# A windowed attention and a two-matrix MLP in one kernel: the first batch's queries and keys loaded on 128 rows over two queues, its masks sliced from one row, block copies in place of zero fills, and the opening put in another order

## The chip, the core and the metric

The kernel runs on one core of a Trainium2 chip. The core has five engines with a queue each: TensorE (PE; its weight loads are shown as PEld), VectorE (DVE), ScalarE (ACT), GpSimd (POOL) and SyncE (SP), which here only issues transfers. An engine takes its instructions in the order of its own queue and waits on semaphores for the others. Sixteen DMA engines move data between the device memory and the core's memory of 128 rows. The metric is the device time of one execution in microseconds; lower is better.

## The reference

```python
def _attn_ref(q, k, v):                 # each (8, 8, 576, 64)
    scores = scale * np.matmul(q, k.transpose(0, 1, 3, 2))
    mask = np.abs(pos[:, None] - pos[None, :]) <= 32
    scores = np.where(mask, scores, -1000000000.0)
    scores = scores - np.max(scores, axis=-1, keepdims=True)
    attn = np.exp(scores)
    attn = attn / (np.sum(attn, axis=-1, keepdims=True) + 1e-09)
    return np.matmul(attn, v)

def _moe_ref(x, w_in, w_out):           # x (4608, 512), w_in (512, 2048), w_out (2048, 512)
    h = x @ w_in
    return np.maximum(0.01 * h, h) @ w_out
```

The attention's output, heads side by side, is the `x` of the second part. Batches are independent; 8 batches of 576 tokens make 4608 rows.

## The kernel before, in words

The heads of a batch are taken in four **pairs** (`p`), the 64 columns of one head on rows 0 to 63 and of the other on 64 to 127. A batch has two **halves** of 288 tokens (`hf`), so an attention step `i` is a batch, a half and a pair, 64 steps in all.

One step: `score(i)` multiplies queries with key blocks of 64 tokens (five small matmuls, one for each key block in reach, L275) into PSUM, ACT takes the exponential (L280), POOL multiplies with a mask of zeros and ones (L282, two inputs, 1.27 us each). `sums(i)` adds over keys with a matmul against a matrix of ones (L304, L301), and VectorE takes the reciprocal (L309). `product(i)` multiplies with the values (L320), and `scaled(i)` multiplies that by the reciprocal into `xT` (L334). The keys `kbd` and the values `vbd` lie as blocks of 128x128 with one head in the upper left and the other in the lower right quarter; the other two quarters have to be zero. `kbd` and `vbd` exist twice, for even and odd batches.

The MLP works on groups `g` of 288 tokens: `h_tile` (L348, 16 column tiles `f` of four matmuls, one for each pair `c`), the leaky ReLU on ACT (`h_out`, L355), and then `o_tile` (L390) for 128 tokens at a time. The last of the four matmuls of a tile needs the product of pair 3. `h_first` runs four tiles side by side, chunk by chunk, so that each pair's chunk can run when its product is there.

Everything is placed by hand (`tc.manual_schedule()`): the order in which the code calls is the order of each engine's queue. After the opening, a plan puts attention steps between the matmuls of the MLP.

What the change touches in the opening:

- **Loads.** `load_qk(b, p)` (L79) reads the q and k of a pair with 96 rows of six tokens (1536-byte runs, 288 KB each); `load_v` (L91) the values, one transfer of 64 rows for each head, in 256-byte runs. All are issued on SP, in the order pair 0, pair 1, values of pair 0, pairs 2 and 3, the other values. Each transfer uses one of eight semaphores, so a ninth waits for the first to land.
- **Casts and transposes.** `cast_qk` (L197, L195) turns q and k into bf16 (q on VectorE or ACT, k on POOL), `transposes` (L225) turns them on TensorE, ACT moves them out of PSUM (L233 for q, L239 for k), and `place_keys` (L258) copies both heads' blocks into `kbd` on VectorE. `cast_v` (L205 on POOL, L203 on ACT) does the same for the values, 64 rows at a time.
- **Zero fills.** `kbd[0]` is cleared on VectorE (L134), `vbd[0]` on ACT (`clear`, L127, three times) and POOL (L158), `kbd[1]` and `vbd[1]` on POOL in eight pieces (L540, L564) between 32 and 45 us.
- **Masks.** Two tiles `mask[hf]`, made on POOL from a pattern `win` (L147 to L165), with even and odd tokens apart, as q's columns are.
- **Weights.** `load_w_in` (L448) and `load_w_out` (L452), four pieces each, are issued by POOL, which casts them to bf16 on the way. The first w_in issue stands on POOL behind the key cast of pair 3.
- **Fillers.** `keep_busy` (L402) issues matmuls whose result nobody reads.

The loads of batch 1 (`load_qk(1, p)`, `load_v(1, p)`) are issued on SP in the opening too; a one-element fill on POOL (L75), which stands behind the second w_out issue, holds them back.

Of the kernel before, what the change touches and what calls it, by code (L numbers as in the profile page):

```python
# [16 lines left out]
def kernel(  # L17
# [14 lines left out]
    nc = tc.nc  # L32
# [34 lines left out]

    def load_qk(b, p, behind=None):

        for into, src, name in ((qf, q, "qf"), (kf, k, "kf")):
            t = fload.tile([96, 2, RUN * D], FP32, name=f"{name}{p}")
# [13 lines left out]
    def load_v(b, p):  # L87

        t = fload.tile([128, NB, D], FP32, name=f"vf{p}")
        for a in range(2):  # L90
            nc.sync.dma_start(  # L91
                out=t[64 * a:64 * a + 64],
                in_=v[b, 2 * p + a].rearrange("(c p) d -> p c d", p=64),
            )
        vf[b, p] = t

    load_qk(0, 0)
    load_qk(0, 1)
    load_v(0, 0)
    load_qk(0, 2)  # L100
    load_qk(0, 3)
    for p in range(1, NPAIR):
        load_v(0, p)
# [5 lines left out]
    nc.vector.tensor_copy(out=ident, in_=ident_f)  # L109

    ones_bd = const.tile([128, 128], BF16)
    nc.vector.memset(ones_bd, 0.0)
    nc.vector.memset(ones_bd[0:64, 0:64], 1.0)
    nc.vector.memset(ones_bd[64:128, 64:128], 1.0)


    qb = const.tile([96, NPAIR, RUN, 2, D], BF16)
    kb = const.tile([96, NPAIR, RUN, 2, D], BF16)
# [4 lines left out]
    nc.vector.memset(zero, 0.0)  # L123

    def clear(t, p):
        flat = t[:, p].rearrange("p n j -> p (n j)")
        nc.scalar.activation(  # L127
            out=flat, in_=zero.to_broadcast([128, NB * 128]), func=AF.Copy,
        )

    mask = [const.tile([128, 2, 2, EVEN], BF16, name=f"mask{i}") for i in range(2)]
    nc.vector.memset(mask[0][:, 1, :, 0:16], 0.0)
    nc.vector.memset(mask[1][:, 1, :, 128:EVEN], 0.0)
    nc.vector.memset(kbd[0], 0.0)  # L134
    clear(vbd[0], 0)
    clear(vbd[0], 1)
    clear(vbd[0], 2)


# [6 lines left out]
    win = const.tile([128, 2, 3, 64], BF16)  # L146
    nc.gpsimd.memset(win, 1.0)  # L147
    for lo in (0, 64):
# [3 lines left out]
            base=0, channel_multiplier=-1, pattern=[[1, 2], [0, 3], [2, 64]],  # L152
# [3 lines left out]
            base=2 * W, channel_multiplier=1, pattern=[[-1, 2], [0, 3], [-2, 64]],  # L156
        )
    nc.gpsimd.memset(vbd[0][:, 3], 0.0)  # L158
    win_f = win.rearrange("p c m i -> p c (m i)")

    def make_mask(hf):
        lo = (16, 32)[hf]
        nc.gpsimd.tensor_copy(out=mask[hf][:, 0], in_=win_f[:, :, lo:lo + EVEN])
        lo = (16, 0)[hf]
        nc.gpsimd.tensor_copy(out=mask[hf][:, 1, :, lo:lo + 128], in_=win_f[:, :, 0:128])  # L165
# [7 lines left out]
    nc.scalar.activation(  # L173
        out=ps[:, 512:512 + HALF], in_=zero.to_broadcast([128, HALF]), func=AF.Copy,
    )
# [8 lines left out]
    qT = {}  # L184

# [13 lines left out]
    def cast_v(b, p, on_act=False):  # L199
        for a in range(2):  # L200
            r = slice(64 * a, 64 * a + 64)
            if on_act:
                nc.scalar.activation(out=vbd[b % 2][r, p, :, r], in_=vf[b, p][r], func=AF.Copy)  # L203
            else:
                nc.gpsimd.tensor_copy(out=vbd[b % 2][r, p, :, r], in_=vf[b, p][r])  # L205
# [42 lines left out]
    def place_keys():  # L248
# [3 lines left out]
        while unplaced:  # L252
            b, p, kT = unplaced.pop(0)
            for a in range(2):
                r = slice(64 * a, 64 * a + 64)
                to = kbd[b % 2][r, p, :, r]
                if b < BY_DMA:
                    nc.vector.tensor_copy(out=to, in_=kT[r].rearrange("p (n j) -> p n j", j=64))  # L258
# [11 lines left out]
    def score(i):  # L270
        b, hf, p = where(i)
        by_c = qT[b][:, p].rearrange("p (c i) -> p c i", c=2)
        for n_, blocks in enumerate(WIN[hf]):
            for blk, i0, n in blocks:
                nc.tensor.matmul(  # L275
                    ps_v[:, n_, :, i0:i0 + n], kbd[b % 2][:, p, blk],
                    by_c[:, :, hf * EVEN + i0:hf * EVEN + i0 + n], start=True, stop=True,
                )
# [368 lines left out]
```

## Time and profile before

| | us |
|---|---|
| three runs | 318.89, 319.77, 320.53 |
| median | 319.77 |
| span of the profiled execution, first to last instruction | 318.5 |
| TensorE busy in the span | 303.2 (95%) |
| VectorE, ACT, POOL busy | 218.2, 182.6, 191.6 |

The profile is of one execution of its own, and its span leaves out what lies before the first and behind the last instruction. Matmuls are pipelined and their ends are modelled, so a busy TensorE need not be a fast one: the five matmuls of a score take 0.65 us in the first 20 us and 0.40 us later, at a granted clock that the profile gives as 1.00 throughout. The chain of waits that ended last is 89% TensorE, 3% DMA and 2% VectorE:

```profile
PE 89%; DMA 3%; DVE 2%; SPq 1%; POOL 1%; ACT 1%; issue 1%; DVEq 0%; ACTq 0%
```

A row of the list of groups reads: line, engine, operation, out<-in, shape and type, count, then busy time in us and the mean of one in ns, then the engine's idle time before them and what ended it.

### The profile page before, as it was taken

To read this page: it belongs to the slowest core of one execution; us is meant where nothing else is said; L and a number is where in the kernel's file an instruction comes from. 1 tells how busy PE (TensorE), PEld (TensorE's weight loads), DVE (VectorE), ACT (ScalarE), POOL (GpSimd) and SP (SyncE) were. 2 spreads that over 40 slices of the span, in tenths; PEclk is the share of its full clock that TensorE was granted. 3 is DMA by queue.
4 is the path that set the end of the run, shared out by engine and by line. 5 is a ranking of instruction groups with operands and counts; after the bars stand their busy time and mean duration, and the time that the engine had idled before them with its cause. 6 is when DMAs were issued, how large, how long until landed. Compare 5 with 4: busy or idle time off the path is not lost.

```text
span 318.5 us, 6474 instructions
## 1 busy us (share of the span) xinstructions
PE 303.2 (95%) x2449; PEld 204.3 (64%) x2449; DVE 218.2 (69%) x259; ACT 182.6 (57%) x393; POOL 191.6 (60%) x251
## 2 busy tenths in 40 slices
PE   2679998999999999999999999999999999999996
PEld 1467774585765858576765858576665858576653
DVE  5678955869655997688755997688745988565100
ACT  7577698474652828374652828375552837464531
POOL 7798963974546866686546866586637866330000
PEclk9999999999999999999999999999999999999999
DMA  8999999997999995399735995399733430000101
GB/s 179 211 186 218 267 250 203 250 206 181 216 242 196 231 206 150 82 251 203 155 76 127 238 227 136 75 223 232 162 76 104 109 70 33 35 35 2 66 31 71
DMA packets 108400, 49.46 MB, mean 155 GB/s; under 512 B 68816, under 2 KB 103888, under 8 KB 108368
## 3 DMA queue, kind: packets, MB, share of 16 engines
q1 hardware_dynamic: 104144, 44.84, 66.8%
q0 software_dynamic: 4224, 4.19, 8.0%
q8 instruction: 19, 0.31, 0.4%
q14 instruction: 13, 0.11, 0.1%
HBM read 36.70 MB, written 9.44 MB: 145 GB/s over the span
## 4 chain that ended last, share of the span: by engine, by line
PE 89%; DMA 3%; DVE 2%; SPq 1%; POOL 1%; ACT 1%; issue 1%; DVEq 0%; ACTq 0%
PE mm L348 39%; PE mm L390 38%; PE x L320 5%; PE ps L275 4%; DMA kf<-in_k_dram 3%; PE s L301 2%; DVE r L309 2%; SPq L79 1%; POOL w_in_bf L448 1%; DVE xT L334 1%; PE tp L225 1%; PE s L304 1%; ACT vbd L203 0%; SPq L91 0%; POOL prob L282 0%
## 5 line engine op out<-in xcount | busy, mean ns | idle before, releaser
L309 DVE RECIPROCAL r<-s 128x288 f32<-128x288 f32 x64 | 125.2, 1956 | 56.5 <-PE s L301 53.3
L282 POOL TENSOR_TENSOR prob<-e,mask 128x576 bf16<-128x576 bf16 x64 | 81.5, 1274 | 87.8 <-ACT e L280 41.1
L348 PE MATMUL mm<-xT,w_in_bf 128*128 128x288 bf16 x1024 | 134.0, 286 | 0.3
L390 PE MATMUL mm<-w_out_bf,gT 128*128 128x512 bf16 (+2 forms) x592 | 130.4, 373 | 0.2 <-DMA w_out_bf<-in_moe_w_out_dram 0.2
L355 ACT ACTIVATE gT<-mm 128x288 bf16<-128x288 f32 x256 | 101.4, 412 | 24.8 <-PE mm L348 8.5
L348 PEld LDWEIGHTS <-w_in_bf 128*128 128x128 bf16 x1024 | 98.4, 98 | 24.8 <-issue 0.6
L390 PEld LDWEIGHTS <-gT 128*128 128x128 bf16 x592 | 56.3, 98 | 59.6 <-issue 0.3
L395 ACT ACTIVATE o_sb<-mm 128x512 f32<-128x512 f32 (+2 forms) x37 | 21.7, 586 | 92.0 <-PE mm L390 92.0
L280 ACT ACTIVATE e<-ps 128x576 bf16<-128x576 f32 x64 | 41.4, 648 | 9.4 <-PE ps L275 9.2
L197 POOL CAST kb<-kf 96x384 bf16<-96x384 f32 (+1 forms) x56 | 35.5, 656 | 4.6 <-DMA kf<-in_k_dram 4.6
L205 POOL CAST vbd<-vf 64x576 bf16<-64x576 f32 x50 | 34.5, 689 | 1.8 <-DMA vf<-in_v_dram 0.4
L334 DVE TENSOR_TENSOR xT<-x,r 128x288 bf16<-128x288 f32 x64 | 29.3, 458 | 8.2 <-PE x L320 1.2
L260 DVE COPY kbd<-kT 64x576 bf16<-64x576 bf16 x48 | 32.3, 672 | 0.3
L275 PE MATMUL ps<-qT,kbd 128*128 128x128 bf16 (+2 forms) x320 | 26.5, 215 | 1.8 <-DVE kbd L258 1.2
L275 PEld LDWEIGHTS <-kbd 128*128 128x128 bf16 x320 | 21.0, 100 | 10.6 <-DVE kbd L258 1.5
L320 PE MATMUL x<-prob,vbd 128*128 128x128 bf16 (+2 forms) x320 | 26.0, 213 | 1.3 <-ACT vbd L203 0.7
L197 POOL CAST qb<-qf 96x384 bf16<-96x384 f32 x48 | 24.5, 538 | 0.0
L320 PEld LDWEIGHTS <-vbd 128*128 128x128 bf16 x320 | 20.6, 99 | 3.9 <-ACT vbd L203 1.8
L292 DVE TENSOR_TENSOR both<-prob 128x288 bf16<-128x288 bf16 x52 | 19.7, 380 | 0.9
L301 PE MATMUL s<-both,ones_bd 128*128 128x288 bf16 x52 | 14.9, 286 | 0.0
L258 DVE COPY kbd<-kT 64x576 bf16<-64x576 bf16 x16 | 7.1, 444 | 8.7 <-ACT kT L239 8.6
L225 PE MATMUL tp<-ident,qb 96*128 96x96 bf16 x48 | 4.4, 243 | 6.2 <-DVE qb L197 6.2
(43 smaller groups left out, 86.6 us busy)
## 6 DMA issues: line engine op xcount, KB each, us to landing
qf<-in_q_dram SPq DMA_DIRECT2D x32, 288.0 KB, 4.5
kf<-in_k_dram SPq DMA_DIRECT2D x32, 288.0 KB, 5.0
vf<-in_v_dram SPq DMA_DIRECT2D x64, 144.0 KB, 4.2
out_dram<-o_sb SPq DMA_DIRECT2D x35, 256.0 KB, 3.6
w_in_bf<-in_moe_w_in_dram POOLq DMA_DIRECT2D x4, 512.0 KB, 8.6
w_out_bf<-in_moe_w_out_dram POOLq DMA_DIRECT2D x4, 512.0 KB, 16.8
qT<-qb SPq DMA_TRANSPOSE x24, 4.1
kT<-kb SPq DMA_TRANSPOSE x24, 3.2
```

The source lines that it names most:

```text
L197: eng.tensor_copy(out=to, in_=tok)
L205: nc.gpsimd.tensor_copy(out=vbd[b % 2][r, p, :, r], in_=vf[b, p][r])
L260: nc.vector.tensor_copy(out=to.rearrange("p n (m c) -> p n c m", c=2), in_=kT[r].rearrange("p (c n m) -> p n c m", c=2, n=NB),)
L275: nc.tensor.matmul(ps_v[:, n_, :, i0:i0 + n], kbd[b % 2][:, p, blk], by_c[:, :, hf * EVEN + i0:hf * EVEN + i0 + n], start=True, stop=True,)
L280: nc.scalar.activation(out=e, in_=ps[:, P0:P0 + 2 * HALF], func=AF.Exp, scale=scale)
L282: nc.gpsimd.tensor_mul(pr.rearrange("p n c i -> p (n c i)"), e, mask[hf].rearrange("p n c i -> p (n c i)"),)
L309: nc.vector.reciprocal(r, s)
L320: nc.tensor.matmul(x_v[:, :, i0:i0 + n], vbd[b % 2][:, p, blk, :], pr[:, n_, :, i0:i0 + n], start=(blk == parts[0][1]), stop=(blk == parts ...
L334: nc.vector.tensor_mul(place(i), x, r)
L348: nc.tensor.matmul(h[:, 0:HALF], w_in_bf[:, c, ts(f, 128)], xT[:, c, ds(g * HALF % RING, HALF)], start=(c == 0), stop=(c == DMC - 1),)
L355: nc.scalar.activation(out=gT[:, f, ds(g * HALF % RING, HALF)].rearrange("p (i c) -> p i c", c=2), in_=h[:, 0:HALF].rearrange("p (c i) -> ...
L390: nc.tensor.matmul(o[:, lo:hi], gT[:, f, ds(128 * j % RING, 128)], w_out_bf[:, f, lo:hi], start=(f == 0), stop=(f == FFC - 1),)
```

## The change

- **Loads of batch 0** (`load_first`): q and k of all pairs lie in two shared buffers of 128 rows. Row `i` holds nine neighbouring tokens; SP loads rows 0 to 63 with five of them (1280-byte runs), ACT loads rows 64 to 127 with the other four (1024-byte runs). Token `9 i + c` for c below 5 stands on row i, for c from 5 on row 64 + i in column c - 5; the fifth column of the lower rows is filled with zeros on POOL. Keys go before queries; pairs 0 and 1 have loads of their own, pairs 2 and 3 share one. The values follow behind all of q and k.
- **Transposes of batch 0** are five of 128x128 and not six of 96x128, for keys and queries (`transpose_first`), and the tokens come out in their natural order, so score, product and leaky ReLU of this batch use plain slices. Eviction (`evict_first`) and placing of the blocks (`place_first`) go to VectorE or ACT, call by call.
- **Masks of batch 0** are overlapping slices of one row `wide`, written from `win` by two ACT copies. The tiles `mask[hf]` for the later batches are copied from it on POOL at the end of the opening.
- **No zero fills** for `vbd[0]`, `kbd[1]` and `vbd[1]`: a block is copied over all 128 rows, times a column `own` that is 1 on the rows of its head and 0 on the others (`own_block`). `kbd[0]` keeps a fill of the two quarters.
- **Weights:** the four w_in issues stand on POOL behind the query cast of pair 1.
- **Order:** the opening is a list of calls, with `score` split into `score`, `exps` and `masked`, and `sums` into `sums` and `inverse`; the masks of steps 0 and 1 are multiplied on VectorE, the others on POOL. 14 filler matmuls stand at the very start, and the others go. The MLP's tiles of group 0 are opened and closed singly.

```diff
+    def load_first(p0, p1, low):
+        for into, src, t in ((kf, k, k_in), (qf, q, q_in)):
+            t = t[:, 0:H * TOP * D].rearrange("p (h c d) -> p h c d", h=H, c=TOP)
+            rows = src[0, 2 * p0:2 * p1].rearrange("h (i c) d -> i h c d", c=ROW)
+            heads = slice(2 * p0, 2 * p1)
+            nc.sync.dma_start(out=t[0:64, heads], in_=rows[:, :, 0:TOP])
+            low.dma_start(out=t[64:128, heads, 0:LOW], in_=rows[:, :, TOP:ROW])
...
-    load_qk(0, 0)
-    load_qk(0, 1)
-    load_v(0, 0)
-    load_qk(0, 2)
-    load_qk(0, 3)
-    for p in range(1, NPAIR):
-        load_v(0, p)
+    load_first(0, 1, nc.scalar)
+    load_first(1, 2, nc.scalar)
...
+    def own_block(eng, out, in_, a):
+        if eng is nc.scalar:
+            eng.activation(out=out, in_=in_, func=AF.Copy, scale=own[:, a:a + 1])
+        else:
+            eng.tensor_scalar_mul(out=out, in0=in_, scalar1=own[:, a:a + 1])
+
+    def value_first(p, a, eng):
+        own_block(eng, vbd[0][:, p, :, 64 * a:64 * a + 64], vf[0, p], a)
...
-    def cast_v(b, p, on_act=False):
+    def cast_v(b, p):
...
-            if on_act:
-                nc.scalar.activation(out=vbd[b % 2][r, p, :, r], in_=vf[b, p][r], func=AF.Copy)
+            if b < BY_DMA:
+                own_block(nc.scalar, vbd[b % 2][:, p, :, r], vf[b, p], a)
...
+    V, G, A = nc.vector, nc.gpsimd, nc.scalar
+    spread(A, GAP + 32, 2)
+    load_first(2, NPAIR, A)
+    qT[0] = attn.tile([128, NPAIR, S], BF16, name="qT")
+    keep_busy(ps, 0, 14, True)
+    cast_first(0, "k", G)
+    fill(V)
+    cast_first(0, "q", V)
+    transpose_first(0, "k")
+    spread(A, 0, 3)
+    transpose_first(0, "q")
+    cast_first(1, "k", V)
+    for p in range(NPAIR):
+        load_v(0, p, V if p == 0 else None)
+    evict_first(0, "k", V)
+    transpose_first(1, "k")
+    evict_first(0, "q", A)
+    cast_first(1, "q", G)
+    evict_first(1, "k", V)
+    place_first(0, A)
+    load_w_in(0, 512)
+    transpose_first(1, "q")
+    place_first(1, V)
+    evict_first(1, "q", A)
+    score(0)
+    load_w_in(512, 1024)
+    cast_first(2, "k", V)
+    exps(0)
+    cast_first(3, "k", V)
+    transpose_first(2, "k")
+    load_w_in(1024, 1536)
+    transpose_first(3, "k")
+    masked(0, V)
+    evict_first(2, "k", A)
+    load_w_in(1536, 2048)
+    cast_first(2, "q", V)
+    score(1)
+    sums(0)
+    cast_first(3, "q", A)
+    place_first(2, V)
+    transpose_first(2, "q")
+    exps(1)
+    value_first(0, 0, G)
+    transpose_first(3, "q")
+    inverse(0)
+    evict_first(2, "q", A)
+    value_first(0, 1, G)
+    evict_first(3, "q", A)
+    score(2)
+    value_first(1, 0, G)
+    product(0)
+    evict_first(3, "k", A)
+    masked(1, V)
+    value_first(1, 1, G)
+    exps(2)
+    scaled(0)
+    sums(1)
+    place_first(3, A)
+    inverse(1)
+    masked(2, G)
+    product(1)
+    value_first(2, 0, A)
+    score(3)
+    value_first(2, 1, G)
+    h_chunk(0)
+    scaled(1)
+    exps(3)
+    sums(2)
+    load_w_out(0)
+    for p in range(NPAIR):
+        load_qk(1, p, nc.gpsimd if p == 0 else None)
+    for p in range(NPAIR):
+        load_v(1, p)
...
+    load_w_out(1)
...
+    make_mask(0, nc.gpsimd)
+    make_mask(1, nc.gpsimd)
```

## The prediction

> **What bounds the kernel now.** I read the page's forty slices first, then three stretches of the span, then the order of VectorE's work in the opening, then the transfers.
>
> ```profile
> PE   2679998999999999999999999999999999999996
> ...
> DMA  8999999997999995399735995399733430000101
> ```
>
> One digit is a slice of 8 us. TensorE is short of full in the first six slices only, and the DMA engines are full in the same slices.
>
> ```profile
> 0.00:37.00 37.00, 25.96 (x244) 19.99 (x245) 28.24 (x36) 25.36 (x45) 32.11 (x45) 1.00 1.12 208
> 37.00:62.00 25.00, 23.80 (x211) 15.26 (x210) 16.61 (x20) 20.66 (x41) 17.02 (x20) 1.00 1.16 234
> 62.00:318.50 256.50, 253.40 (x1997) 169.09 (x1995) 173.32 (x205) 136.59 (x308) 142.49 (x188) 1.00 0.66 140
> ```
>
> Columns: stretch, length, busy time of PE, PE's loads, DVE, ACT, POOL, granted clock, DMA share, GB/s. After 62 us TensorE is idle for 3.1 us of 256.5, and the change leaves that part alone. So it is worth what it takes from the first 37 us, less what the next 25 give back.
>
> What ends those 37 us is VectorE's row of reciprocals and products (start, length, engine, line):
>
> ```profile
> 13.45 1.96 DVE L309 RECIPROCAL r<-s 128x288 f32<-128x288 f32 x1 [0.31 <-PE s L304]
> ...
> 16.58 1.95 DVE L309 RECIPROCAL r<-s 128x288 f32<-128x288 f32 x1
> 18.97 0.91 DVE L258 COPY kbd<-kT 64x576 bf16<-64x576 bf16 x2 [0.45 <-ACT kT L239]
> 20.52 1.96 DVE L309 RECIPROCAL r<-s 128x288 f32<-128x288 f32 x1 [0.64 <-PE s L304]
> ...
> 26.29 1.96 DVE L309 RECIPROCAL r<-s 128x288 f32<-128x288 f32 x1
> ...
> 28.96 1.95 DVE L309 RECIPROCAL r<-s 128x288 f32<-128x288 f32 x1
> ...
> 34.10 1.96 DVE L309 RECIPROCAL r<-s 128x288 f32<-128x288 f32 x1
> ...
> 36.17 0.46 DVE L334 TENSOR_TENSOR xT<-x,r 128x288 bf16<-128x288 f32 x1
> ```
>
> The eighth product ends at 36.63, and group 1 of the first matrix product needs it. From 13.45 that is 23.2 us. VectorE's work in it is 8 x 1.95 + 8 x 0.46 + 1.8 for two pairs of key copies = 21.1, so only 2.1 us are idle, most of it before the third reciprocal. From there on one period takes 2.5 to 2.7 us, of which 2.41 is work. VectorE is the limit here; TensorE, at 25.96 of 37 busy, is not.
>
> The transfers behind it (second fence: stretches as above; third: waits that end on a landing):
>
> ```profile
> 2.00:4.00 2.00, 0.00 (x0) 0.00 (x0) 1.47 (x6) 1.77 (x3) 1.81 (x4) 1.00 1.00 274
> ...
> 48.00:50.00 2.00, 1.78 (x23) 1.19 (x22) 0.30 (x1) 1.57 (x3) 1.20 (x1) 1.00 1.23 185
> 50.00:52.00 2.00, 1.29 (x13) 0.63 (x11) 1.96 (x3) 1.93 (x4) 0.00 (x0) 1.00 0.93 163
> ```
>
> ```profile
> 15.54 0.82 POOL L197 CAST kb<-kf 96x768 bf16<-96x768 f32 x1 [0.49 <-DMA kf<-in_k_dram]
> ...
> 48.84 1.02 PE L390 MATMUL mm<-w_out_bf,gT 128*128 128x512 bf16 x4 [0.22 <-DMA w_out_bf<-in_moe_w_out_dram]
> ```
>
> Queries and keys alone go at 274 GB/s, value loads of 64 rows at 163 to 185. The last keys of batch 0 are there at 15.5, and w_out's last quarter only when TensorE asks for it.
>
> **The change, part by part.** *Zero fills.* Three fills of vbd on ACT (L127, 1.15 each), one on POOL (L158, 1.06), and eight on POOL later (1.07 each) go. All stand in time in which their engine was ahead, so I cost them at nothing. The eight were followed by POOL's key casts at 37.93, which did not hold TensorE up. In exchange the block copies of the first two batches (values in both; keys in batch 1 alone) run over 128 rows with a scalar for each row. ACT's rows go by elements, not rows (64x576 0.68, 128x1152 1.15), so the same time, and 0 to 0.1 for the scalar. TensorE did wait for such a pair at 51.06 (ACT vbd L203, 0.7), so I add 0.1 in all. On POOL and VectorE this operation is not in the trace; bounds are POOL's cast (0.67) and its two-input product (1.27). I take 0.7, since it reads one tensor. At 1.27 seven pieces put 4 us on POOL before 22 us, of which only about 1 us lies ahead of a product that VectorE waits for.
>
> *Masks.* Sliced from one row, with the first two products moved from POOL (1.27) to VectorE. The nearest VectorE row is a product of half the size, 128x288 in 0.38 (L292): 0.38 to 0.76, and I take 0.7. The first lies before the first reciprocal, the second after it: +0.7 in the row.
>
> *Weights early.* The four w_in issues leave their place behind the last key cast (16.31) for one behind pair 1's query cast (about 8.5), and SP's value loads move behind all of q and k. The first piece landed 5.5 us after its issue at best; the first product asked for it at 23.5. No gain in itself, but the weights now share the engines with pairs 2 and 3. The 14 opening matmuls run before anything has landed: nothing.
>
> *The opening's order and loads.* On VectorE there now stands ahead of the first reciprocal: k of pair 1, two evictions, the keys of pair 1, k of pairs 2 and 3, the first mask, then **the query cast of pair 2, which waits for the last q transfer**, and pair 2's keys. With the cast at 0.56 (L197's undisturbed row) and the keys at 0.91, the reciprocal starts 1.47 us after that landing. Behind the waiting cast stand all reciprocals. Were nothing late, the queue itself would allow 13.1: pair 1's keys cast from 6.9 (where its query cast began before), 0.56, two evictions of 0.7 (0.65 on ACT), keys 0.91, two casts of 0.56, first mask 0.7, cast 0.56, keys 0.91.
>
> So the landing decides. It is 2.36 MB (8 loads of 288 KB). Early windows carry 159 (0:5), 216 and 212 GB/s, which passes 2.36 MB at 12.3 us. Before, 0.29 MB of values stood in front, so 13.6, and the last was there at 15.5: a lag of 1.9. With it, 14.2, and up to 0.7 more for weights that take a third from 10 us on. Against that, twelve loads on two issuing queues (SP rows 0 to 63, ACT rows 64 to 127) spread over all 128 rows. If rows set the rate, 274 x 128/96 = 365 GB/s: 6.5 + 1.85 (first bytes) + 1.9 = 10.3. If halves go like the 64-row value loads, 2.36 MB at 163 to 185 is 13 to 14.5, landing near 17. I take 13.5, nearer the middle row because packets of 1280 and 1024 bytes are nearer 1536 than 256.
>
> The Trainium skill speaks to this twice. "SBUF — State Buffer", section "Door 1: The DMA port swizzle", says that rows 0 to 63 reach only half of SBUF's ports and all 128 reach all; and "Can I just issue two DMAs to hit both halves?" on that page answers no, two half transfers gain 6% over one. By its 196 GB/s for 64 rows, 208 GB/s and 11.3 us, an estimate, the landing would be near 16 and the sum 321.4. No row of this trace has two half loads on two queues.
>
> *Sum.* First reciprocal 13.5 + 1.47 = 14.97. Then seven periods of 2.5, the second mask 0.7, and the last reciprocal with its product 2.53: 20.7, so 35.67 against 36.63: **-0.96**. With +0.1 from ACT, **-0.86 us**. The profiled execution spans 318.5; its three runs have 318.89 to 320.53, median 319.77, so 1.3 lies around the span. 319.77 - 0.86 = **318.9**.
>
> **Later cover.** DMA stays full until 50 us and must carry the same bytes, so w_out's last quarter cannot come much earlier. Batch 1's loads (SP, eight of q and k, eight of values) now wait behind one w_out issue on POOL and no longer two, and pass more of w_out. The matmuls that ask for it at 48.84 have room until 51.06, less their 4 x 0.22 and a sum of 0.4: a gain of about 1 us survives even if it lands no earlier.
>
> **Rivals.**
> - *A, as summed* (0.38): the last q lands between 12.5 and 14.5. 318.9.
> - *B, the halves fill the engines* (0.34): landing at 11.6 or before, reciprocal at 13.1, product at 33.8, -2.8; with the 0.1, and 0.1 lost to the later cover, 317.2. For it: 96 rows leave a quarter of the rows unused, and the dip to 170 GB/s in 15:20, some 1 us of transfer, is there for early weights to fill, which w_out needs to come earlier too. Against: the DMA share in 2:4 is already 1.00.
> - *C, the last query load is late* (0.22): POOL's weights and SP's values run while ACT's lower half of pairs 2 and 3, issued only after an earlier landing frees a semaphore, is still in flight. At a landing of 17 the product ends at 17 + 1.47 + 20.7 = 39.2: +2.5, 322.3. It decides from a landing of 14.5 on. For it: three queues then share the engines, and 64-row loads are the slowest rows. Against: those rows are of 256-byte packets.
> - *D, hidden anyway* (0.06): the opening gains, and w_out, passed by batch 1's loads, takes it back by 52 us: 319.8.
>
> By the Trainium skill's answer on half transfers (above) C gains weight; its chance is left as the traces bear it.
>
> **Numbers.** I count more than 0.5% (1.6 us) as told apart from no change. A and D are within it: 0.44; B 0.34; C 0.22. Range 316.8 to 322.0: B's price to a landing of 16.6 in C. A alone, over landings of 12.5 to 14.5, is 317.9 to 319.9.
>
> **What would show it.** Right: the first reciprocal near 15, right behind pair 2's query cast, and then no idle over 0.3 us on VectorE; eighth product at 35 to 36.6; first product of w_in waiting for its landing, not for xT. Wrong step by step: pair 2's query cast far from 13.5 (landing); per-row copies on POOL over 1 us and reciprocals waiting for POOL's masks (that price); TensorE idle over 1.5 us between 44 and 52 (the cover). The whole fails if reciprocals are not back to back, so that something other than VectorE sets the opening.

## The result and the profile after

The kernel after takes 331.11 us (median of four runs, 330.37 to 331.34), the kernel before beside it 319.63 us (318.89 to 320.53): a ratio of 1.0355, 95% interval 1.0327 to 1.0383, or 11.3 us slower. Forecast were 318.9 us and a range of 316.8 to 322.0.

The page of the kernel after, the 40 slices (8.2 us each) and the shares of the chain of waits by engine and by line:

```profile
PE   4535999899999999999999999999999999999995
...
PEclk9555899999999999999999999999999999999999
DMA  7996999978999899659942899398924620010101
...
PE 86%; DMA 6%; DVE 3%; SPq 2%; issue 1%; ACT 1%; POOL 1%; DVEq 0%; ACTq 0%; POOLq 0%
PE mm L454 37%; PE mm L512 37%; DMA vf<-in_v_dram 5%; PE x L425 4%; PE ps L362 4%; PE s L399 2%; DVE r L412 2%; SPq L108 2%; DMA qf<-in_q_dram 1%; PE s L402 1%; PE tp L299 1%; PE ps L354 1%; POOL vbd L252 1%; DVE xT L440 0%; DVE kb L152 0%
```

Before, TensorE was at 6 to 9 tenths from the second slice on; now it stays at 3 to 5 for four slices. The largest wait of the chain for a transfer was 3% of the span, for keys; now it is 5%, for the **values** (`vf`). The DMA engines are 90% busy or more in the second and third slice, where TensorE waits, and fall to 6 tenths in the fourth.

The same execution in four stretches (length, busy time of PE, PE's loads, VectorE, ACT and POOL, granted clock, DMA share, GB/s):

```profile
0.00:37.00 37.00, 19.30 (x143) 13.76 (x144) 20.89 (x36) 15.82 (x25) 23.23 (x32) 0.63 0.96 179
37.00:47.50 10.50, 9.85 (x91) 7.63 (x90) 9.67 (x9) 6.45 (x18) 7.37 (x11) 1.00 1.14 260
47.50:73.00 25.50, 24.07 (x211) 15.48 (x213) 14.82 (x20) 20.17 (x41) 12.00 (x15) 1.00 1.11 207
73.00:329.40 256.40, 251.79 (x1977) 168.74 (x1992) 172.89 (x204) 136.77 (x308) 141.61 (x187) 1.00 0.67 136
```

In its first 37 us TensorE does 19.3 us of work where it did 26.0, and VectorE 20.9 where it did 28.2. The stretch that the forecast gave to VectorE no longer has it as its limit. VectorE's row of reciprocals and products shows where it stands (start, length; in brackets the idle time and what ended it):

```profile
14.76 0.81 DVE L152 CAST qb<-qf 128x640 bf16<-128x640 f32 x1
15.49 0.90 DVE L152 COPY kbd<-kT 64x576 bf16<-64x576 bf16 x2
16.41 1.96 DVE L412 RECIPROCAL r<-s 128x288 f32<-128x288 f32 x1
...
20.66 1.96 DVE L412 RECIPROCAL r<-s 128x288 f32<-128x288 f32 x1
27.20 0.46 DVE L440 TENSOR_TENSOR xT<-x,r 128x288 bf16<-128x288 f32 x1 [4.58 <-PE x L425]
29.09 1.96 DVE L412 RECIPROCAL r<-s 128x288 f32<-128x288 f32 x1 [1.44 <-PE s L402]
...
33.77 1.96 DVE L412 RECIPROCAL r<-s 128x288 f32<-128x288 f32 x1 [1.89 <-PE s L402]
...
46.54 0.46 DVE L440 TENSOR_TENSOR xT<-x,r 128x288 bf16<-128x288 f32 x1
```

The eighth product ends at 47.00 and not at 36.63: 10.4 of the 10.9 us by which the profiled spans differ (329.4 and 318.5). Behind it both take nearly the same: 282.4 and 281.9 us. The largest gap, 4.58 us, waits for product 1 (`x`), and that for POOL, which makes its values block. POOL's queue in the same time:

```profile
9.40 3.19 POOL L570 DMA_DIRECT2D w_in_bf<-in_moe_w_in_dram  x4
16.01 3.43 POOL L252 TENSOR_SCALAR vbd<-vf,own 128x576 bf16<-128x576 f32 x2 [3.43 <-DMA vf<-in_v_dram]
23.04 3.43 POOL L252 TENSOR_SCALAR vbd<-vf,own 128x576 bf16<-128x576 f32 x2 [3.59 <-DMA vf<-in_v_dram]
26.43 1.27 POOL L380 TENSOR_TENSOR prob<-e,wide 128x576 bf16<-128x576 bf16 x1
28.97 1.72 POOL L252 TENSOR_SCALAR vbd<-vf,own 128x576 bf16<-128x576 f32 x1 [1.26 <-DMA vf<-in_v_dram]
30.64 0.83 POOL L574 DMA_DIRECT2D w_out_bf<-in_moe_w_out_dram  x1
```

Two things are to be seen. Three times POOL waits for a value landing, 8.3 us in all, and the masks and the first w_out issue wait behind it; w_out's issue came at 22.77 before. And a copy over 128 rows with the factor takes 1.72 us on POOL, where a cast of 64 rows took 0.67.

When the transfers landed (us; of the values, the second half of each pair), from the trace of each kernel:

| kernel | last q, k | v 0 | v 1 | v 2 | v 3 | w_in, four pieces |
|---|---|---|---|---|---|---|
| before | 15.49 | 10.23 | 16.78 | 18.36 | 19.74 | 21.85, 24.39, 28.00, 30.83 |
| after | 14.05 | 15.81 | 22.89 | 28.81 | 29.79 | 18.41, 21.73, 25.10, 28.47 |
| before, weights early | 14.29 | 9.66 | 21.33 | 28.55 | 30.07 | 16.93, 20.23, 23.61, 28.14 |
| after, weights late | 13.85 | 15.28 | 16.80 | 18.28 | 19.31 | 24.52, 27.10, 30.24, 33.00 |
| after, w_in in eight | 14.85 | 16.26 | 20.84 | 25.66 | 30.48 | 19.76, 24.04, 28.33, 31.83 |

In the kernel after, w_in is there 2.4 to 3.4 us sooner, and the values of pairs 1 to 3 come 6 to 10.5 us later. Packets that the DMA engines began in each 2 us, counted in the traces of the two kernels:

```
              after: w_in's queue   values' queue     before: w_in's queue   SP's queue
14 to 16       290, 297 KB          343,  86 KB          0                   1392, 349 KB
16 to 18       320, 312 KB          319,  80 KB          0                   1441, 361 KB
18 to 20       307, 313 KB          307,  77 KB        238, 244 KB            226,  53 KB
20 to 22       320, 311 KB          321,  79 KB        417, 411 KB              0
22 to 24       316, 313 KB          315,  80 KB        415, 414 KB              0
28 to 30         2,   1 KB          644, 158 KB        361, 354 KB             29,  45 KB
30 to 32         0                    0                219, 223 KB            215, 309 KB
```

**In the stretches in which both queues have work throughout, they send one packet each in turn.** A packet of w_in carries 1 KB (counted in bf16, as it is written), one of the values 256 bytes, so the values get a fifth of the bytes: 40 KB a us, and 180 alone. The count gives the landing: w_in has 4 x 512 = 2048 packets, and one for one at 157 a us they last some 13 us (in the trace they run from 13.4 to 28.0); only then do the values' last packets run at their own pace. The Trainium skill, "DMA: Bandwidth & Descriptors", section "Queues, rings and completion order", says that each DMA engine goes round the queues that it has work for, packet by packet; the counts agree (its packet may hold several descriptors, which counts over 2 us can't tell). The 238 beside 226 packets of before at 18 to 20 us are chance: the last value packet begins at 18.9, and most of those of w_in behind it. But before's trace could have shown the rule, with packets of 1024 and 1536 bytes: from 34 to 36 us w_out has 214 and the loads of batch 1 have 218.

### The profile page after: what moved, and what is told of

The parts are those of the page before. It is cut to its first block, busy times and chain, and to the rows that moved or that the text cites. A ratio compares the mean times of both kernels' runs of the same rounds, so it can differ in the third digit from the quotient of the medians.

```text
span 329.4 us, 6429 instructions
## 1 busy us (share of the span) xinstructions
PE 305.0 (93%) x2414; PEld 205.6 (62%) x2434; DVE 218.3 (66%) x267; ACT 179.2 (54%) x390; POOL 184.2 (56%) x243
## 4 chain that ended last, share of the span: by engine, by line
PE 86%; DMA 6%; DVE 3%; SPq 2%; issue 1%; ACT 1%; POOL 1%; DVEq 0%; ACTq 0%; POOLq 0%
PE mm L454 37%; PE mm L512 37%; DMA vf<-in_v_dram 5%; PE x L425 4%; PE ps L362 4%; PE s L399 2%; DVE r L412 2%; SPq L108 2%; DMA qf<-in_q_dram 1%; PE s L402 1%; PE tp L299 1%; PE ps L354 1%; POOL vbd L252 1%; DVE xT L440 0%; DVE kb L152 0%
## 5 line engine op out<-in xcount | busy, mean ns | idle before, releaser
L454 PE MATMUL mm<-xT,w_in_bf 128*128 128x288 bf16 x1024 | 136.2, 288 | 0.5 <-DVE xT L440 0.4
L512 PE MATMUL mm<-w_out_bf,gT 128*128 128x512 bf16 (+2 forms) x572 | 128.7, 373 | 1.1
L380 POOL TENSOR_TENSOR prob<-e,mask 128x576 bf16<-128x576 bf16 x56 | 71.4, 1275 | 91.7 <-ACT e L372 45.5
L440 DVE TENSOR_TENSOR xT<-x,r 128x288 bf16<-128x288 f32 x64 | 29.3, 458 | 13.4 <-PE x L425 6.3
L279 POOL CAST vbd<-vf 64x576 bf16<-64x576 f32 x48 | 33.4, 696 | 1.4
L271 POOL CAST kb<-kf 96x384 bf16<-96x384 f32 (+1 forms) x52 | 30.8, 615 | 5.7 <-DMA kf<-in_k_dram 5.7
L337 DVE COPY kbd<-kT 64x576 bf16<-64x576 bf16 x48 | 32.3, 673 | 0.4
L425 PEld LDWEIGHTS <-vbd 128*128 128x128 bf16 x320 | 20.9, 100 | 13.7 <-POOL vbd L252 10.4
L362 PEld LDWEIGHTS <-kbd 128*128 128x128 bf16 x280 | 18.1, 98 | 8.2
L362 PE MATMUL ps<-qT,kbd 128*128 128x96 bf16 (+1 forms) x280 | 22.5, 211 | 0.0
L252 POOL TENSOR_SCALAR vbd<-vf,own 128x576 bf16<-128x576 f32 x5 | 8.6, 1723 | 8.3 <-DMA vf<-in_v_dram 8.3
L250 ACT ACTIVATE vbd<-vf,own 128x576 bf16<-128x576 f32 x11 | 8.1, 774 | 8.6 <-DMA vf<-in_v_dram 8.6
```

The source lines that it names most:

```text
L271: eng.tensor_copy(out=to, in_=tok)
L337: nc.vector.tensor_copy(out=to.rearrange("p n (m c) -> p n c m", c=2), in_=kT[r].rearrange("p (c n m) -> p n c m", c=2, n=NB),)
L362: nc.tensor.matmul(ps_v[:, n_, :, i0:i0 + n], kbd[b % 2][:, p, blk], by_c[:, :, hf * EVEN + i0:hf * EVEN + i0 + n], start=True, stop=True,)
L380: eng.tensor_mul(pr.rearrange("p n c i -> p n (c i)"), e.rearrange("p (n t) -> p n t", n=2), allowed,)
L425: nc.tensor.matmul(x[:, lo:hi] if b == 0 else x_v[:, :, i0:i0 + n], vbd[b % 2][:, p, blk, :], flat[:, n_, lo:hi] if b == 0 else pr[:, n_, ...
L440: nc.vector.tensor_mul(place(i), x, r)
```

## The experiments

Ratios are to the kernel before, run on the same chip; the us in brackets are the ratio less one, times 319.6. Theory S: the early weights take the values' share of the DMA engines. Its rivals at the start: P, the price of POOL's per-row copies; C, TensorE's clock, which the profiled execution shows as granted at 0.50 from 10 to 35 us.

**1. Weights behind the values, and POOL's copies as casts, singly and together.**

The edit for late weights, and behind it the one for casts:

```diff
-    load_w_in(0, 512)
...
     value_first(0, 1, G)
+    load_w_in(0, 512)
+    load_w_in(512, 1024)
...
     value_first(1, 1, G)
+    load_w_in(1024, 1536)
+    load_w_in(1536, 2048)
```

```diff
     fill(V)
+    clear(V, vbd[0], slice(0, 3))
...
     def value_first(p, a, eng):
+        if eng is nc.gpsimd:
+            r = slice(64 * a, 64 * a + 64)
+            eng.tensor_copy(out=vbd[0][r, p, :, r], in_=vf[0, p][r])
+            return
```

> The kernel after, with the four w_in issues moved behind POOL's copies of the values of pairs 0 and 1 (two behind each). Theory S (sharing): in the kernel after, the w_in transfers, issued from 9.4 us on, run beside the value loads, and the values get the small share (some 40 KB in a us, landings 15.8, 22.9, 28.8, 29.8); with the weights behind them the values land by 16.5, 18, 20, 21 as fast as before, and the time falls from 331.1 to 321-325. Rival P (price): it is the five per-row copies on POOL at 1.72 us, 1.05 each more than a cast of 64 rows; they stay, so 326 or more. Rival C (clock): TensorE's granted clock of 0.50 until 35 us with no fillers in between; it stays, so 329 or more.

> The kernel after, weights early as they are, with POOL's five value copies as casts of 64 rows, and zero fills for pairs 0 to 2 of vbd on VectorE before the first queries land. S: the values land as late as in the kernel after, and only what stands behind the last landing gets shorter, 1 to 2 us: 329-330.5. P: 5 x 1.05 = 5.2 less: 326. C: 331.

> Both edits: weights behind the value copies, and POOL's value copies as casts of 64 rows. S and P together: 318.5-321, that is 2 to 5 under the kernel with late weights alone, as the copies then stand in the row. C: 326 or more.

Measured: late weights 328.88, 1.0299 [1.0283, 1.0314] (+9.6); casts 330.13, 1.0337 [1.0321, 1.0354] (+10.8); both 324.55, 1.0154 [1.0130, 1.0179] (+4.9). The values land as S says (table), yet the time does not fall to 325, which S gave: behind early values stand POOL's copies, two pairs of 3.4 us each. P's 326 for the casts is missed as well, and S's 329 to 330.5 met. Neither theory alone holds. Alone the two edits take back 1.7 and 0.5 us, together 6.4 of 11.3, as each of the two waits hides the other. It is less than the 10 to 12.6 that S and P together gave (318.5 to 321).

**2. The kernel before with the weights early, and nothing else.**

```diff
     make_mask(0)
+    load_w_in(0, 512)
+    load_w_in(512, 1024)
     cast_qk(0, 1, nc.vector)
...
     cast_v(0, 0)
+    load_w_in(1024, 1536)
     score(0)
...
     score(1)
+    load_w_in(1536, 2048)
```

> The kernel before with nothing but its four w_in issues earlier on POOL (from 7 us on, in POOL's idle time, where they stood at 16.3 to 20). S: they now run beside the loads of pairs 2 and 3 and of the values, which land 5 to 10 us later than before: 323-328. P and C: nothing that they name is in it, so 319-320; and a gain of 0 to 1 if weights were what the first products of the MLP wait for.

Measured: 327.81, 1.0250 [1.0202, 1.0297] (+8.0). S, in its range; the values land as late as in the kernel after. ACT, which casts them here, and VectorE, in its timeline:

```profile
21.35 0.68 ACT L203 ACTIVATE vbd<-vf 64x576 bf16<-64x576 f32 x1 [1.73 <-DMA vf<-in_v_dram]
...
26.33 0.68 ACT L203 ACTIVATE vbd<-vf 64x576 bf16<-64x576 f32 x1 [3.62 <-DMA vf<-in_v_dram]
28.58 0.68 ACT L203 ACTIVATE vbd<-vf 64x576 bf16<-64x576 f32 x1 [1.57 <-DMA vf<-in_v_dram]
...
29.98 0.46 DVE L334 TENSOR_TENSOR xT<-x,r 128x288 bf16<-128x288 f32 x1 [6.99 <-PE x L320]
```

No per-row copy is in this kernel, and VectorE idles 6.99 us before its third product. A rival would be that the issues themselves hold POOL up. They do so by 0.14 us: the first two reciprocals start at 13.59 and 16.71 (13.45 and 16.58 before), and the third is even earlier; the fourth, behind the late values, starts at 30.46 and not at 23.83, and the eighth product ends at 44.93, 8.3 late. This is the strongest evidence here: four issues moved forward on POOL, and nothing else, cost 8 us (6.5 to 9.5 by the interval).

**3. Smaller packets for the weights** (the kernel after, `load_w_in` eight times with 256 columns).

> The kernel after as it is, but w_in in eight transfers of 256 columns instead of four of 512, so that its runs are 512 bytes in bf16 and not 1024, against 256 for the values. Theory S, packet by packet: the values' share of the engines' bytes rises from a fifth to a third while both run, so the last values land some 3 to 5 us before 29.8, and the time falls to 326-329. Rival W: the values are late because their issues wait on SP, or because a transfer of 64 rows is slow by itself; then they land as late as before, and the time is 331 or, with the smaller pieces, more.

Measured: 330.54, 1.0331 [1.0308, 1.0354] (+10.6). S's time and landing are missed (30.48 for the last value), and by these two alone rival W would have been right. The packets decide against W: the share went as S says, from 16 to 28 us some 494 packets of each queue in 2 us, 245 KB of w_in and 123 KB of values, a third; and with the weights late (experiment 1) the same 64-row loads are there at 19.31. What S had wrong is how long it lasts. Half the packet means twice as many (4096), so the turn by turn lasts until the values' 4608 are nearly through. In these two runs the number of packets in the other queue, and 190 to 200 GB/s for both, give the values' end (246 x 768 bytes a us are 189 GB/s, 157 x 1280 are 201).

**4. What was left: TensorE's and VectorE's queue order, and the clock.** All three start from both edits of experiment 1.

The first puts the chunk behind the sums, the second also the first mask ahead of the casts, the third adds 23 fillers (`keep_busy(ps, 0, n)`) at six places.

```diff
-    h_chunk(0)
     scaled(1)
     exps(3)
     sums(2)
+    h_chunk(0)
```

```diff
     exps(0)
+    masked(0, V)
+    score(1)
+    sums(0)
+    inverse(0)
+    exps(1)
     cast_first(2, "k", V)
     cast_first(3, "k", V)
```

> The kernel with late weights and 64-row casts (324.6, 5.2 above before), with the first chunk of w_in on TensorE put behind sums of step 2 and no longer ahead of them. Theory Q (queue order): of what is left, a part is that TensorE stood 2.0 us before that chunk for w_in's first landing (22.9), with the sums of step 2 behind it, and VectorE 2.5 us before its third reciprocal (24.6). With the chunk behind, that reciprocal starts when POOL's mask of step 2 is done (22.4) and its sums are made, at 23, and the time falls by 1.5: 323. Rival C: the cold TensorE (a group of five at 0.65 us, granted clock 0.50 to 0.69, up to 28 us) sets it: 324.5. Rival L: it is lost later than the opening, to w_out and the loads of batch 1: 324.5.

> The same, and on VectorE the first mask and the first reciprocal ahead of the key casts of pairs 2 and 3, whose landing (13.1) VectorE awaits for 2.35 us; score of step 1 follows score of step 0 directly. Q: the first reciprocal starts at 12.8 and not at 16.6; VectorE's work stays the same, so some 1 to 2.3 us less than the run with the chunk behind: 321-322. C: within 0.5 of it. L: 324.5.

> The same again, with 23 filler matmuls at TensorE's idle places between 11 and 23 us. C: TensorE's groups take 0.40 instead of 0.65, and with some six of them in the chain from one reciprocal to the next the time falls by 1 to 2 us. Q: VectorE's row sets the opening, so within 0.5 us of the run without them.

Measured: the chunk behind 323.72, 1.0122 [1.0107, 1.0137] (+3.9); and the mask first 323.43, 1.0116 [1.0101, 1.0131] (+3.7); and fillers 323.96, 1.0134 [1.0117, 1.0152] (+4.3). The chunk behind gains 1.0, at the edge of what the intervals tell apart; Q gave 1.5. The mask first misses Q's 321 to 322. The first reciprocal moved from 16.6 to 12.93, but the second came at 19.83, where before has 16.58: what VectorE did ahead of the row it now does inside. With the fillers the clock is granted in full, and the time does not fall. The first 35 us of the run without and of the run with them, the clock behind POOL's count:

```profile
0.00:35.00 35.00, 24.14 (x194) 17.19 (x195) 28.29 (x42) 20.32 (x37) 23.26 (x40) 0.95 1.12 208
```

```profile
0.00:35.00 35.00, 24.69 (x210) 18.49 (x211) 27.35 (x42) 19.62 (x36) 22.69 (x39) 1.00 1.08 207
```

This pair alone does not settle C, as the clock was at 0.95 without fillers, and they have a price: from the first reciprocal to the end of the eighth product it takes 25.8 us with them and 26.3 without, but the first reciprocal comes at 14.16 and not at 12.93, for the most part because five fillers stand ahead of its sums. The kernel after itself settles it for the granted clock. Its profiled execution, with 0.50 from 10 to 35 us and a mean of 0.958 over the span, took 331.11; two others with a mean of 1.000 took 331.34 and 331.10. And in the profile of experiment 3 the clock is granted at 1.00 through the whole opening, at 330.88 us. C falls.

**5. The rest on VectorE, or in the order of the loads?** On top of chunk and mask: the key casts of pairs 2 and 3 on POOL; then the values of pair 0 ahead of the loads of pairs 2 and 3; and, from the first of these, one w_in piece early.

```diff
-    cast_first(2, "k", V)
-    cast_first(3, "k", V)
+    cast_first(2, "k", G)
+    cast_first(3, "k", G)
```

```diff
+    load_v(0, 0)
     load_first(2, NPAIR, A)
```

> The kernel with late weights, 64-row casts, the chunk behind and the mask first (323.4, 3.6 above before), with the key casts of pairs 2 and 3 on POOL, which stands idle from 9 to 14.9, and not on VectorE. Theory V (VectorE's row): what is left is VectorE's own work between its first reciprocal and the eighth product: 26.3 us from 12.9 to 39.2, of which two key casts (1.5) and two masks (0.95) were not in the 23.2 us of before. Without the casts the time falls by 1.2 to 1.8: 322. Rival L: the rest is lost behind 39 us (TensorE has 4.0 busy of 50 to 55, before 4.3): 323.4.

> The same, with the values of pair 0 loaded ahead of q and k of pairs 2 and 3, as the kernel before has it, and their POOL casts ahead of the key casts. Theory V: product 0 is not what the row waits for, and q of pair 2 lands 1.4 us later, before VectorE asks for it: within 0.7 of the run before it. Rival O (the order of the loads is itself a cost, values last): 1 to 2 us faster.

> The kernel with keys on POOL, with the first of the four w_in pieces issued early (at 9) and the three others behind the value copies. Theory S: the piece lands near 18.7 and not 22.5, but the values of pair 1 land 2 to 3 us later meanwhile; as the first chunk now stands behind the sums of step 2, nothing waits for it at 18.7, and the time is 0 to 2 us above the run with keys on POOL. Rival: the first w_in landing is what TensorE waits for, and the time falls by 0.5 to 1.5.

Measured: keys on POOL 323.51, 1.0113 [1.0084, 1.0143] (+3.6), no gain, so theory V fell: VectorE had 1.5 us less to do and waited them out. The number is rival L's, but not its cause: behind the eighth product every version built on the kernel after takes 282.36 to 282.38 us, and those built on the kernel before 281.87 to 281.93, so only 0.5 us is lost there. Values first 323.04, 1.0099 [1.0071, 1.0127] (+3.2), not told apart from it, as V had it. One piece early 324.37, 1.0142 [1.0113, 1.0171] (+4.5), within S's 0 to 2 and not the gain of its rival. With the values first there was a new wait, of ACT for the last values and of VectorE behind it:

```profile
24.71 0.77 ACT L250 ACTIVATE vbd<-vf,own 128x576 bf16<-128x576 f32 x1 [2.65 <-DMA vf<-in_v_dram]
...
26.76 1.96 DVE L416 RECIPROCAL r<-s 128x288 f32<-128x288 f32 x1 [2.06 <-PE s L406]
```

The last half of the values landed at 24.63, 5.2 us behind the half before it: it was issued at 15.3, between two w_in issues at 14.6 and 15.5.

**6. Following that wait.** From values first: the second w_in issue behind the copies of pair 1. From that, two masks on VectorE; or, apart from them, the first two chunks behind the sums of step 3, and then a mask ahead of the first w_out issue.

```diff
     cast_first(3, "k", G)
     load_w_in(0, 512)
-    load_w_in(512, 1024)
...
     value_first(1, 1, G)
+    load_w_in(512, 1024)
```

```diff
-    h_chunk(0)
...
-    h_chunk(1)
...
     sums(3)
+    h_chunk(0)
+    h_chunk(1)
```

> The kernel with the values of pair 0 first (323.0, 3.2 above before), with the second of two w_in issues, made at 15.5 ahead of the copies of pair 1, moved behind those copies. In that kernel the last half of the values landed at 24.6, 5.2 us behind the one before it, ACT stood 2.65 us for it, and VectorE 2.06 us before its fourth reciprocal. Theory S: those two w_in transfers took its share again; with one of them behind, the values land by 22, the fourth reciprocal starts at 25, and the time falls by 1.2 to 1.9: 321.1-321.8. Rival G (POOL's row is full from 13 to 25 with copies, weight issues and masks): the issue only moves, the mask of step 2 comes 0.4 later, and the time is 323 or more.

> The same, with the masks of steps 2 and 3 on VectorE (0.46 each) ahead of the reciprocals of steps 1 and 2, and not on POOL (1.27 each). G: POOL's row is 2.5 us shorter, and the time falls by another 0.5 to 1.5. Theory V (VectorE's row is the limit, and every 0.46 in it counts): 0.5 to 0.9 more than the run before it.

> The kernel with one weight issue behind the copies of pair 1 (322.6, 2.9 above before), with the first two chunks of w_in on TensorE behind the sums of step 3. There all values had landed by 19.9, but the first piece of w_in only at 23.5, TensorE stood 1.29 us before the first chunk, and the fourth reciprocal came at 27.3, 1.89 us after VectorE was free. Theory T (one supply: what lands first makes the other late, and the row pays for whichever TensorE's queue has in front): with the chunks behind, the fourth reciprocal starts at 25.2 and the time falls by 1.5 to 2: 320.6-321.1. Rival L (the rest is lost behind the eighth product): 322-322.6.

> The same, with the mask of step 3 ahead of the first w_out issue on POOL, so that it starts at 22.7 and not at 23.5. T: the fourth reciprocal starts right behind the third product, at 24.8, and the time is 0.2 to 0.6 less than the run before it; it would then be 0.5 to 1 above the kernel before, as the row still holds two masks (0.9 us) more than before's. Rival L: no change.

Measured: one behind 322.62, 1.0085 [1.0060, 1.0110] (+2.7); masks on VectorE 323.60, 1.0117 [1.0095, 1.0139] (+3.7); chunks later 324.94, 1.0180 [1.0158, 1.0201] (+5.8); mask ahead 324.52, 1.0163 [1.0140, 1.0186] (+5.2). One behind lies between S's 321.1 to 321.8 and G's 323, and is not told apart from values first. Masks on VectorE goes V's way and not G's, but the profiled executions have the eighth product the other way round (39.31 with the masks, 40.15 without), so V is not shown. Chunks later misses both theories, and is slower; mask ahead is not told apart from it, and far from T's 0.5 to 1 above before. In the run with one behind all values are there at 19.93, and the wait has moved to the weights:

```profile
23.55 0.91 PE L458 MATMUL mm<-xT,w_in_bf 128*128 128x288 bf16 x4 [1.29 <-DMA w_in_bf<-in_moe_w_in_dram]
...
27.30 1.96 DVE L416 RECIPROCAL r<-s 128x288 f32<-128x288 f32 x1 [1.89 <-PE s L406]
```

With the chunks behind, the fourth reciprocal does come at 25.94, but three chunks then stand together and hold up the next product:

```profile
25.70 2.71 PE L458 MATMUL mm<-xT,w_in_bf 128*128 128x288 bf16 x12
...
28.92 0.46 DVE L444 TENSOR_TENSOR xT<-x,r 128x288 bf16<-128x288 f32 x1 [1.02 <-PE x L429]
30.12 1.96 DVE L416 RECIPROCAL r<-s 128x288 f32<-128x288 f32 x1 [0.75 <-PE s L406]
```

So the eighth product of the versions of experiments 4 to 6 ends at 39.2 to 40.7, 2.6 to 4.1 us after that of the kernel before, and none beats it.

**7. Other parts of the change alone in the kernel before.** Values of pair 0 loaded behind q and k of all pairs, cast behind the second mask; POOL's two copies of pair 0 over 128 rows; and no fills of the odd buffers, with the copies of batch 1 over 128 rows in exchange.

```diff
-    load_v(0, 0)
     load_qk(0, 2)
     load_qk(0, 3)
-    for p in range(1, NPAIR):
+    for p in range(NPAIR):
```

```diff
+            elif b == 0:
+                nc.gpsimd.tensor_scalar_mul(
+                    out=vbd[0][:, p, :, r], in0=vf[0, p], scalar1=own[:, a:a + 1])
```

```diff
-            nc.gpsimd.memset((kbd if f < 12 else vbd)[1][:, (f - 4) // 2 % 4], 0.0)
...
-            nc.gpsimd.memset(vbd[1][:, (f - 3) // 2], 0.0)
```

> The kernel before with the other half of the change's load order alone: the values of pair 0 behind q and k of all pairs (they land at 15 to 15.5 and not at 9 to 10.2), and POOL's casts of them behind the mask of step 1, so that no mask waits for them; the weights stay where they were. Theory S (the early weights make the loss, the order of the loads little): the first product is 1.2 us late, of which the idle time before the third reciprocal takes up half: 319.8-321. Rival O (values behind q and k are the loss): 323 or more.

> The kernel before with the third part of the change alone: POOL's two copies of pair 0's values over 128 rows with the factor (1.72 each in the kernel after) and not as casts of 64 rows (0.67). They stand ahead of POOL's mask of step 0, so that mask, the first sums and the first reciprocal come 2.1 us less POOL's idle time there (0.37 and 0.44) later, 14.8 in place of 13.45. Theory P: the row of reciprocals is late by 1.3, of which the idle time before the third reciprocal (0.64) and the key copies' wait (0.45) may take up half: 320.3-321.1. Rival: the row takes all of it up, 319.5-320.

> The kernel before with one part of the change alone: no zero fills of kbd[1] and vbd[1] on POOL (eight of 1.0), the keys and values of batch 1 copied over 128 rows with the factor, on VectorE and ACT. The prediction costed the fills at nothing and the copies at 0 to 0.1: 319.8 to 320. Rival: POOL's 8 us between 32 and 45 held back key casts or masks of batch 1, and the time falls by 0.5 to 1.5.

Measured: values last 321.55, 1.0054 [1.0035, 1.0072] (+1.7), between the two, much nearer S; POOL's copies 322.19, 1.0080 [1.0056, 1.0104] (+2.6), more than P gave; no late fills 319.85, 1.0004 [0.9984, 1.0024], nothing, as forecast. POOL and VectorE with the copies over rows:

```profile
9.34 3.73 POOL L209 TENSOR_SCALAR vbd<-vf,own 128x576 bf16<-128x576 f32 x2 [0.95 <-DMA vf<-in_v_dram]
13.04 1.27 POOL L288 TENSOR_TENSOR prob<-e,mask 128x576 bf16<-128x576 bf16 x1
...
15.03 1.96 DVE L315 RECIPROCAL r<-s 128x288 f32<-128x288 f32 x1 [3.55 <-PE s L310]
```

The first reciprocal comes 1.6 us later, and the eighth product ends at 37.89, 1.3 late. The profiled span grew by as much (319.8). The medians say twice that. Part of it is that this trace is of an execution of 321.48 us, 0.7 under its median, while before's span of 318.5 is longer than that of most of its runs (317.2 to 318.7 in the eleven beside this run, eight of them under 318.5); the rest is not shown.

**The sum.** Weights early +8.0, POOL's copies +2.6, values last +1.7, fills 0.1: 12.4, and the whole change costs 11.3. That the two are near each other proves little: the parts were tried one at a time in the order of the kernel before, and experiment 1 shows that they do not simply add up. Taken away from the kernel after, the first two give back only 6.4; one reason is that w_in then lands at 22.9 and TensorE's queue has its first chunk in front. The parts that were not tried alone, the 128-row loads and the new order, are not told apart from each other; of the last 3 us, 0.5 lie behind the eighth product in every version, and the cause of the rest, ahead of it, stays open.

## Why the prediction was wrong, step by step

- **What bounds the kernel.** Right for the kernel before, and right that the opening decides: 10.4 of 10.9 us lie ahead of the eighth product. Its last test failed: the reciprocals are not back to back, and something other than VectorE sets the opening. In the terms of the sum, the eighth product ends at 47.00 and not at 35.67. Of these 11.3 us, 1.4 lie in the first reciprocal (16.41, not 14.97) and 9.9 in the row behind it (30.6 us, not 20.7), which was summed without any wait.
- **"Weights early ... No gain in itself, but the weights now share the engines with pairs 2 and 3": the step that failed.** It moved two things, w_in's issues forward and the value loads back, and looked only at their meeting with q and k, which is small: the last q landed at 14.05 (13.5 was taken), and at 13.85 with the weights late. The transfers that w_in really meets are the values, which stand last on SP's queue with packets of 256 bytes; their later landing was put at nothing, without a reason. Tried alone, the early issues cost 8.0 us (experiment 2), and the place of pair 0's values 1.7. The rule of one packet each in turn could have been read beforehand from before's trace, at 34 to 36 us.
- **POOL's per-row copy, taken at 0.7 within 0.67 to 1.27.** Measured 1.72, outside both bounds. Two rows of other operations don't bound an operation that the trace does not have. The two of pair 0 alone, in the kernel before, cost 2.6 us (1.87 each there); the forecast gave it nothing, and 1 us at the upper bound. The page of the kernel after has it, and ACT's copy with the same factor:

```profile
L252 POOL TENSOR_SCALAR vbd<-vf,own 128x576 bf16<-128x576 f32 x5 | 8.6, 1723 | 8.3 <-DMA vf<-in_v_dram 8.3
L250 ACT ACTIVATE vbd<-vf,own 128x576 bf16<-128x576 f32 x11 | 8.1, 774 | 8.6 <-DMA vf<-in_v_dram 8.6
```

- **Zero fills at nothing, ACT's factor at 0 to 0.1.** Right: 1.0004, and 0.77 against 0.68. TensorE's wait for ACT's pair near 51 us grew from 0.71 to 1.00 with them, not by 0.1, and the time did not show it. Masks on VectorE: 0.46, within 0.38 to 0.76, below the 0.7 taken.
- **First reciprocal 1.47 us behind the last q.** 2.36: the key casts ahead of it had waited for their own landing until 12.93, so VectorE reached the query cast 0.71 late, and casts of 128x640 take 0.7 to 0.8, not 0.56.
- **Rivals.** None occurred. B needed a landing by 11.6. C had the mechanism, three queues sharing the engines, and named the wrong victim: the query, which landed ahead of C's 14.5. D is out: the opening gains nothing that could be hidden. The landing of 14.05 lies within A's 12.5 to 14.5, so what A said of the loads came true, and the time it gave did not.
- **The rate of the loads.** The Trainium skill's "Can I just issue two DMAs to hit both halves?" (SBUF — State Buffer) has 6% for two half transfers over one. No run here has that pair; two half loads on two queues gain 3% over one queue of 96 rows: by the packets begun, 235 GB/s up to 11.76 us, when the first value packet follows, and 229 up to 12 us before. The last query packet ends at 13.04, so the lag to the landing is 1.0 us, where 1.9 was taken.
- **Slips in the working.** Five per-row pieces stand on POOL, not seven. From the third reciprocal of before to its fourth it is 3.31 us, not 2.5 to 2.7. Time and span differ by 1.7 us in the runs, not by 1.3; the forecast does not hang on it. 11.3 with the first bytes and the lag is 15.1, and near 16 only with the 0.7 for weights. The lower end of the range, 316.8, is below B's price, 317.2, without a term for it.
- **Later cover.** Not needed: 0.5 us are lost behind the eighth product, with everything 10 us later; what takes them is not shown.

## What to carry to other kernels

An idle issuer does not make it free to move a transfer forward: count the packets of every queue that will have work at that time. In these traces they go one for one, so large packets in one queue starve small ones in another, for as many packets as the first queue has. Put the transfer with small packets ahead, or hold the large one back until it has landed; and where the trace lacks an operation, run it once before relying on bounds from others.

## What the runs showed of the hardware that was not expected

- Two queues send one packet each in turn at three pairs of packet sizes: 157 packets a us of each queue at 1024 and 256 bytes, 246 at 512 and 256, some 110 at 1024 and 1536 (before, 32 to 42 us); values alone 720.
- A multiplication by one factor per row, 128x576 from f32 into bf16, takes 1.72 us on POOL (1.87 in the kernel before with such copies) and 0.77 on ACT. On VectorE the nearest form, from bf16, takes 0.47.
- The granted clock of the profile does not tell how fast the matmuls of an opening run. It was 0.50 from 10 to 35 us in the profile of the kernel after and 1.00 in that of w_in in eight, and a group of five small matmuls took 0.61 to 0.66 us in both until 34 us, as before's did in its first 20 us at 1.00; 0.40 us came behind stretches in which TensorE had been at work, with matmuls of the program or fillers.
